# Token chunks of up to 512 columns, no widened copy of the pooled attention, and another split of the weights' rounding

## The chip, the cores and the metric

The kernel runs on one core of a Trainium2 chip. The metric is the device time of one execution in microseconds; of several runs the median counts.

## What is computed

Attention over 8 batches, 8 heads, 576 positions and head dimension 64, and a feed-forward layer on its 4608 tokens. The attention is the sum of two parts: one on `q`, `k`, `v` averaged over groups of four positions, its result repeated four times, and one in which each position sees its neighbours at a distance under 4.

```python
q_d = q.reshape(B, H, Sd, factor, D).mean(axis=3)   # k_d, v_d alike
out_d = sm_attn(q_d, k_d, v_d)
out_up = np.repeat(out_d, factor, axis=2)
mask = np.abs(pos[:, None] - pos[None, :]) < factor
scores = np.where(mask, scale * np.matmul(q, k.transpose(0, 1, 3, 2)), -1e9)
out_local = np.matmul(softmax(scores), v)
x = (out_up + out_local).transpose(0, 2, 1, 3).reshape(B * S, H * D)   # 4608 x 512
h = x @ w_in                      # 512 x 2048
g = np.maximum(0.01 * h, h)
return g @ w_out                  # 2048 x 512
```

## The kernel before

**Number format.** To keep float32 accuracy, each operand of the feed-forward layer is split into a high part (rounded to the format `F32R`) and a low part (what is left), and each product is three matmuls: high by high, low by high, high by low. In the code a trailing `h` or `l` names the part: `gh`, `gl`, `woh`, `wol`; `wi` holds both parts of `w_in`.

**Chunks.** The tokens are columns of all feed-forward matmuls. `plan()` cuts them into `CHUNKS`. Chunk 0 has 512 columns, all of batch 0, whose local attention is made as banded matmuls on TensorE (lines 756 to 831). The other batches are laid out as 9 columns of 64 tokens each (in a batch, "column" j holds the positions that are j modulo 9). `SIZES` gives the number of such columns in each chunk: `(3,) + (6,) * 10`, so chunk 1 has the last 64 tokens of batch 0 and 3 × 64 = 192 more, 256 together, and ten chunks have 384. The last two are made by Strassen's scheme with seven products in place of eight (`finale()`, line 1343).

**Steps.** `STEPS` is the list of feed-forward steps (chunk, first column, last column, f), where f is one of 16 slices of 128 of the 2048 hidden units. A step is twelve up matmuls into a tile `hp` (`up_proj`, line 1060: four slices of x by three products), the leaky ReLU (`leaky`: ScalarE writes `gh` at line 1071 and the exact value at 1072, VectorE the difference `gl` at 1074), and twelve down matmuls into four accumulators of PSUM (`down_proj`, line 1098). Chunk 0 is cut into two halves of 256 columns (`TOP`): the first half runs ahead through f 0 to 7, then the halves alternate, so that the first half is at f + 8 when the second is at f. That spreads over time the moment at which each slice of the weights is first wanted.

**Weights.** `convert(f, k)` makes the parts of slice f of `w_in` (k = 0) or `w_out` (k = 1) from a loaded tile: ScalarE moves the first half word (line 335), VectorE merges it (337), the high part is rounded by ScalarE (348, `w_in`) or by VectorE (345, `w_out`), and the low part is VectorE's subtraction (350). This takes place in the first 120 us, while chunk 0's steps run.

**Local attention of the batches from 1 on.** For each three columns and each half of the heads: GpSimd multiplies q by seven shifted k (line 896), VectorE sums over d (902), some small softmax work follows, GpSimd multiplies by v (969) and VectorE sums (975) into a tile `xloc`. `widen()` lets ScalarE copy the pooled attention's result `outd`, repeated four times, into a tile `up` (line 994, two copies for one part). `landing()` transposes `xloc` on TensorE into a PSUM tile `pt` (1007), adds `up` to it on VectorE (1013), writes the high part of x on ScalarE (1028) and the low part on VectorE (1030):

```python
t = yield from op("DVE", 270 * n, t, tu)
nc.vector.tensor_tensor(out=xv, in0=xv, in1=upv, op=ALU.add)
```

**What sets the order.** All parts are Python generators that run under a planner, the class `Order`. A generator asks for a buffer (`slot`), waits for a named event, and asks for an engine with an estimated duration (`op`); of the generators that are ready, the one with the lowest rank gets the engine next. So the order of every engine's instructions is fixed when the program is built, from estimated costs (`COST`) and ranks; on the chip each engine runs its list in order and waits for semaphores. The x chunks lie in two buffers by parity (`x0`, `x1`), `hp` and `pt` have two each, `gh` and `gl` three each, `xloc` and `prod` two each.

## Time and profile before

| what | value |
|---|---|
| three runs | 911.55, 911.89, 912.01 us |
| their median | 911.89 us |
| profiled execution, span | 910.3 us |
| instructions in the span | 16167 |
| matmuls of 256 columns in up_proj and down_proj | 1152 |
| matmuls of 384 columns in up_proj and down_proj | 3264 |

The profiled execution has no time of its own beside its span; the median of the runs is 1.6 us above that span. PE is TensorE, PEld its weight loads, DVE VectorE, ACT ScalarE, POOL GpSimd, SP SyncE. A row of grouped instructions gives the line, the engine, the operation, the output and input with their shapes, the count, then the busy time in us and the mean ns of one, then the idle time of the engine before them and what ended it. TensorE's rows overlap, since matmuls are pipelined: what one costs is seen from start to start.

### The profile page before, as it was taken

How to read it: one execution, taken by the hardware profiler on the slowest of the kernel's cores; microseconds unless marked ns; L12 is line 12 of the kernel's file. 1: busy time of each engine (PE TensorE's matmuls, PEld its weight loads, DVE VectorE, ACT ScalarE, POOL GpSimd, SP SyncE). 2: the span in 40 equal slices, each digit the busy share in tenths (PEclk: the TensorE clock that was granted, in tenths of full speed). 3: DMA queues.
4: the chain of work that ended last, by engine and by line, in shares of the span. 5: the costliest groups of instructions: out<-in, count | busy, mean ns of one | idle time of the engine just before them, and what ended most of it. 6: DMA issues, size and time to landing. Idle time of an engine off the chain costs nothing. (4 is left out here: it accounts for less than half of the span.)

```text
span 910.3 us, 16167 instructions
## 1 busy us (share of the span) xinstructions
PE 897.6 (99%) x6129; PEld 870.5 (96%) x6129; DVE 610.1 (67%) x887; ACT 460.9 (51%) x1277; POOL 625.9 (69%) x308
## 2 busy tenths in 40 slices
PE   8999999999999999999999999999999999999998
PEld 4789999999999999999999999999999999999998
DVE  6899889888878977875746863762863755533322
ACT  5788567666455634554324553533413425455332
POOL 4221299989989999967974964982993986787100
PEclk9999999999999999999999999999999999999999
DMA  9786566657646644652522751630431410100001
GB/s 294 257 297 240 174 205 207 199 161 216 199 124 200 210 117 121 207 176 64 153 86 76 213 161 27 176 106 27 122 113 45 122 53 1 36 1 1 1 35 36
DMA packets 61774, 119.68 MB, mean 131 GB/s; under 512 B 7248, under 2 KB 24016, under 8 KB 61696
## 3 DMA queue, kind: packets, MB, share of 16 engines
q1 hardware_dynamic: 61696, 118.65, 42.0%
q8 instruction: 48, 0.79, 0.3%
q14 instruction: 30, 0.25, 0.1%
HBM read 109.18 MB, written 9.44 MB: 130 GB/s over the span
## 5 line engine op out<-in xcount | busy, mean ns | idle before, releaser
L1060 PE MATMUL hp<-x,wi 128*128 128x384 f32 (+1 forms) x2112 | 367.4, 323 | 4.5 <-DVE gl L1074 3.6
L1060 PEld LDWEIGHTS hp<-x,wi 128*128 128x128 f32 x2112 | 338.3, 189 | 8.8 <-DVE gl L1074 4.8
L969 POOL TENSOR_TENSOR prod<-v,s 128x1344 f32<-128x1344 f32 x84 | 261.8, 3124 | 62.2 <-DVE xloc L975 57.6
L896 POOL TENSOR_TENSOR prod<-q,k 128x1344 f32<-128x1344 f32 x84 | 265.9, 3171 | 52.7 <-DVE s L902 27.0
L1098 PE MATMUL acc<-gh,woh 128*128 128x384 f32 (+1 forms) x768 | 252.3, 329 | 0.0
L1098 PE MATMUL acc<-gh,wol 128*128 128x384 f32 (+1 forms) x768 | 247.1, 322 | 0.1
L1098 PE MATMUL acc<-gl,woh 128*128 128x384 f32 (+1 forms) x768 | 246.8, 321 | 0.0
L1071 ACT ACTIVATE gh<-hp 128x384 fp32r<-128x384 f32 (+1 forms) x184 | 85.3, 464 | 223.0 <-PE acc L1098 216.8
L1074 DVE TENSOR_TENSOR gl<-hp,gh 128x384 fp32r<-128x384 f32 (+1 forms) x184 | 95.2, 518 | 133.6 <-ACT hp L1072 130.0
L1098 PEld LDWEIGHTS acc<-gh,woh 128*128 128x128 f32 x768 | 144.8, 189 | 2.5 <-issue 2.0
L1098 PEld LDWEIGHTS acc<-gh,wol 128*128 128x128 f32 x768 | 144.8, 188 | 0.5 <-DVE wol L350 0.5
L1098 PEld LDWEIGHTS acc<-gl,woh 128*128 128x128 f32 x768 | 145.0, 189 | 0.0
L902 DVE TENSOR_REDUCE s<-prod 128x21 f32<-128x1344 f32 x84 | 129.3, 1541 | 13.9 <-POOL prod L896 13.9
L975 DVE TENSOR_REDUCE xloc<-prod 128x192 f32<-128x1344 f32 x80 | 123.4, 1543 | 5.1 <-POOL prod L969 5.1
L1072 ACT ACTIVATE hp<-hp 128x384 f32<-128x384 f32 (+1 forms) x184 | 84.4, 459 | 0.0
L1013 DVE TENSOR_TENSOR pt<-pt,up 128x384 f32<-128x384 f32 x42 | 37.6, 895 | 24.6 <-PE pt L1007 22.4
L994 ACT COPY up<-outd 128x576 f32<-128x576 f32 x84 | 52.1, 672 | 0.0
L425 DVE TENSOR_REDUCE v_d<-vs 128x128 f32<-128x512 f32 (+1 forms) x56 | 37.6, 671 | 5.9 <-DMA vs<-in_vrb_dram 5.0
L1028 ACT CAST x<-pt 128x384 fp32r<-128x384 f32 x38 | 18.4, 484 | 35.7 <-DVE pt L1013 35.7
L783 POOL TENSOR_TENSOR xloc<-xloc,lst 128x280 f32<-128x280 f32 (+1 forms) x8 | 7.3, 919 | 27.0 <-ACT pd L512 12.2
L1170 POOL TENSOR_TENSOR sr<-sr 128x256 f32<-128x256 f32 x32 | 23.8, 758 | 0.9
L1170 POOL TENSOR_TENSOR sr<-wi 128x512 f32<-128x512 f32 x16 | 20.6, 1291 | 3.9 <-DVE pt L1013 3.8
(231 smaller groups left out, 1028.4 us busy)
## 6 DMA issues: line engine op xcount, KB each, us to landing
k<-in_kb_dram SPq DMA_DIRECT2D x84, 288.0 KB, 3.3
v<-in_vb_dram SPq DMA_DIRECT2D x84, 288.0 KB, 2.9
qk<-in_qkt_dram SPq DMA_DIRECT2D x32, 576.0 KB, 4.9
q<-in_qb_dram SPq DMA_DIRECT2D x84, 96.0 KB, 2.0
vs<-in_vmb_dram SPq DMA_DIRECT2D x28, 256.0 KB, 2.8
out_dram<-olot SPq DMA_DIRECT2D x36, 192.0 KB, 2.0
...
```

What stands on the lines that cost most here:

```text
L425: nc.vector.tensor_reduce(out=v_d[:rows, k], in_=vs, axis=AX.X, op=ALU.add)
L896: nc.gpsimd.tensor_tensor(out=prv, in0=q[:, a - j0:z - j0].unsqueeze(2).to_broadcast([128, n, W, D]), in1=view(k, (a - j0) * D, [[D, n], [ ...
L902: nc.vector.tensor_reduce(out=s[:, u, p, a - j0:z - j0], in_=prv, axis=AX.X, op=ALU.add)
L969: nc.gpsimd.tensor_tensor(out=prv, in0=view(v, 0, [[1, nj], [nv, D], [1, W]]), in1=s[:, p, :nj].unsqueeze(2).to_broadcast([128, nj, D, W]) ...
L975: nc.vector.tensor_reduce(out=xl_t[:, :nj, p], in_=prv, axis=AX.X, op=ALU.add)
L994: nc.scalar.copy(out=up[:, pp], in_=outd[b][:, 2 * u + pp].unsqueeze(2).to_broadcast([128, SD, FAC]))
L1060: nc.tensor.matmul(hp[:, :n], w[h][:, ws], x[:, c], start=c + j == 0, stop=c == NC - 1 and j == 2)
L1071: nc.scalar.activation(out=gh[:, :n], in_=hp[:, :n], func=AF.Prelu, alpha=0.01)
L1072: nc.scalar.activation(out=hp[:, :n], in_=hp[:, :n], func=AF.Prelu, alpha=0.01)
L1074: nc.vector.tensor_tensor(out=gl[:, :n], in0=hp[:, :n], in1=gh[:, :n].bitcast(F32), op=ALU.subtract)
L1098: nc.tensor.matmul(acc[:, a:z], w[h][:, es], g[:, :n], start=(a, f, j) == (0, 0, 0), stop=f == NF - 1 and j == 2, skip_group_check=ch == 0)
L1170: (nc.vector if eng == "DVE" else nc.gpsimd).tensor_tensor(out=out, in0=in0, in1=in1, op=alu)
```

## The change

1. `SIZES` becomes `(3, 6, 6, 6, 6, 8, 8, 8, 6, 6)`: chunk 1 stays at 256 columns, then come four chunks of 384, three of 512 and the last two of 384. There are 11 chunks in place of 12. Parts of three columns stay, and one may now land in two chunks, so `plan()` keeps for each part the list of its landings. Both x buffers are 512 columns wide; `x1`, which first serves as three staging tiles for the weights, has room for a fourth, and that takes the weights' head tiles.
2. Chunk 0: the first half of the columns runs f 0 to 7 as before. After that, behind each step of the second half for f comes one step of all 512 columns for f + 8. Two half steps share one pair of `gh`, `gl` tiles (`HALF`, `pairs`).
3. `widen()` and its tile `up` are gone. `landing()` adds `outd` to the PSUM tile directly. Since the repeat by four can't be written as one view across a column's tokens, a column takes one or two adds (`RUNS`: 15 for nine columns, 5 for three).
4. `w_out`'s high part is always rounded on ScalarE, and the low parts of the first ten slices (`SHARED`) are subtracted on GpSimd.
5. For Strassen's T4 the buffers are other ones: its two parts lie in what chunk tiles leave free, so that a matmul reads it as three pieces of 128 columns (`Cut`).

```diff
-SIZES = (3,) + (6,) * 10
+SIZES = (3, 6, 6, 6, 6, 8, 8, 8, 6, 6)
...
+SHARED = 10
...
-    parts = {b: [] for b in range(BANDED, B)}
+    parts = {b: [(j, j + MAXSEG, []) for j in range(0, BLK, MAXSEG)] for b in range(BANDED, B)}
     g = 0
     for i, n in enumerate(SIZES):
         mine, z, c0 = [], g + n, 0 if i else S - 512
         while g < z:
             b, j = divmod(g, BLK)
-            room = min(BLK - j, z - g)
-            m = -(-room // -(-room // MAXSEG))
+            _, j1, lands = parts[b + BANDED][j // MAXSEG]
+            m = min(j1 - j, z - g)
             mine.append((b + BANDED, j, j + m, c0))
-            parts[b + BANDED].append((i + 1, j, j + m, c0))
+            lands.append((i + 1, j, j + m, c0))
...
-for f in range(NF):
-    STEPS += [(0, *TOP[1], f)] + [(0, *TOP[0], f + LEAD)] * (f + LEAD < NF)
+for f in range(LEAD):
+    STEPS += [(0, *TOP[1], f), (0, 0, TOP[1][1], f + LEAD)]
...
+HALF = [i for i, (_, a, z, _) in enumerate(STEPS) if z - a == 256]
+HALF = {i: divmod(n, 2) for n, i in enumerate(HALF)}
...
+def runs(j):
+    at = [(BLK * r + j) // FAC for r in range(FAC)]
+    cuts = [0] + [r for r in range(1, FAC) if at[r] != at[r - 1] + 2] + [FAC]
+    return [(r0, r1, at[r0]) for r0, r1 in zip(cuts, cuts[1:])]
+
+
+RUNS = [runs(j) for j in range(BLK)]
...
-    edge_sb = const.tile([128, BLK, W], F32, name="edge_sb")
+    edge_sb = axp.tile([128, BLK, W], F32, name="edge_sb")
...
-    heads = [axp.tile([128, DM], I32, name=f"head{i}") for i in range(bufs["head"])]
+    stage = [wk.tile([128, bufs["stage"] + 1, HALFS * DM], U16, name="x1", tag="x1", bufs=bufs["x1"])]
+    heads = [stage[0][:, bufs["stage"], i * 2 * DM:(i + 1) * 2 * DM].bitcast(I32) for i in range(bufs["head"])]
...
-        s = yield from slot(*(("prod", "up") if f < FREE else ("stage2",) if FSPLIT < f < LSPLIT else ()), "stage")
+        s = yield from slot(*(("prod",) if f < FREE else ("stage2",) if FSPLIT < f < LSPLIT else ()), "stage")
...
-        if k:
-            t = yield from op("DVE", 330, t, lock=True)
-            nc.vector.tensor_copy(out=hi, in_=tf)
+        t = yield from op("ACT", 512, t)
+        nc.scalar.copy(out=hi, in_=tf)
+        if k and f < SHARED:
+            t = yield from op("POOL", 512, t)
+            nc.gpsimd.tensor_tensor(out=lo, in0=tf, in1=hi.bitcast(F32), op=ALU.subtract)
         else:
-            t = yield from op("ACT", 512, t)
-            nc.scalar.copy(out=hi, in_=tf)
-        t = yield from op("DVE", 512, t, lock=True)
-        nc.vector.tensor_tensor(out=lo, in0=tf, in1=hi.bitcast(F32), op=ALU.subtract)
+            t = yield from op("DVE", 512, t, lock=True)
+            nc.vector.tensor_tensor(out=lo, in0=tf, in1=hi.bitcast(F32), op=ALU.subtract)
...
-        both = sb(s_x, [128, 2, NC, XMAX[i % 2]], F32R)[:, :, :, :CHUNKS[i][1]]
+        whole = sb(s_x, [128, 2, NC, 512], F32R)
+        both = whole[:, :, :, :CHUNKS[i][1]]
+        if i == LAST - 1:
+            fin["spare"] = whole[:, :, :, EN:].rearrange("p h c n -> p (h c) n")
...
-        od.spawn(90 + 10 * b + j0 + 0.5 * u, landing(i, b, j0, u, a, z, c0, s_x, xl_t, t))
-
-    ups = {}
-
-    def widen(i, b, j0, j1, u):
-        to = yield from wait(("pooled", b, 2 * u))
-        to = max(to, (yield from wait(("pooled", b, 2 * u + 1))))
-        tx = yield from wait(("xbuf", i))
-        yield from wait(("upturn", ORD[b, j0, u]))
-        s_u = yield from slot("up")
-        od.signal(("upturn", ORD[b, j0, u] + 1))
-        up = sb(s_u, [128, 2, SD, FAC], F32)
-        t = yield from op("ACT", 2 * S, s_u.t, to, times=2)
-        for pp in range(2):
-            nc.scalar.copy(out=up[:, pp], in_=outd[b][:, 2 * u + pp].unsqueeze(2).to_broadcast([128, SD, FAC]))
-        od.signal(("read", b), t)
-        ups[b, j0, u] = up
-        od.signal(("up", b, j0, u), max(t, tx))
-        s_u.free((yield from wait(("upread", b, j0, u), len(pieces(j0, j1)))))
-
-    def landing(i, b, j0, u, a, z, col, s_x, xl_t, t):
+        for k, (i, a, z, col) in enumerate(lands):
+            od.spawn(90 + 10 * b + a + 0.5 * u, landing(i, b, j0, u, a, z, col, s_x, xl_t, t, k == len(lands) - 1))
+
+    def landing(i, b, j0, u, a, z, col, s_x, xl_t, t, last):
         n = z - a
-        tu = yield from wait(("up", b, j0, u))
+        to = max((yield from wait(("pooled", b, 2 * u))), (yield from wait(("pooled", b, 2 * u + 1))))
+        to = max(to, (yield from wait(("xbuf", i))))
         s_b = yield from slot("pt")
         xps = bank(s_b)
         t = yield from pe(0.11 * n, t, s_b.t)
         for m in range(n):
-            nc.tensor.transpose(xps[:, m * 128:(m + 1) * 128], xl_t[:, m].rearrange("p a d -> p (a d)"), id_sb)
-        s_x.free(t)
-        up = ups[b, j0, u]
+            nc.tensor.transpose(xps[:, m * 128:(m + 1) * 128], xl_t[:, a - j0 + m].rearrange("p a d -> p (a d)"), id_sb)
+        if last:
+            s_x.free(t)
         xv = xps[:, :n * 128].rearrange("p (j c t) -> p c j t", j=n, c=2)
-        upv = view(up, a, [[S, 2], [1, n], [BLK, NBLK]])
-        t = yield from op("DVE", 270 * n, t, tu)
-        nc.vector.tensor_tensor(out=xv, in0=xv, in1=upv, op=ALU.add)
-        od.signal(("upread", b, j0, u), t)
+        adds = [(m, *run) for m in range(n) for run in RUNS[a + m]]
+        t = yield from op("DVE", 128 * n, t, to, times=len(adds))
+        for m, r0, r1, o in adds:
+            part = view(xps, m * 128 + r0, [[NBLK, 2], [FAC, NBLK // FAC], [1, r1 - r0]])
+            nc.vector.tensor_tensor(out=part, in0=part, in1=view(outd[b], 2 * u * SD + o, [[SD, 2], [BLK, NBLK // FAC], [2, r1 - r0]]), op=ALU.add)
+        od.signal(("read", b), t)
...
+    pairs = {}
+
     def leaky(i, n, s_h, hp, t):
-        s_g, s_l = (yield from slot("gh")), (yield from slot("gl"))
-        gh, gl = sb(s_g, [128, OMAX], F32R), sb(s_l, [128, OMAX], F32R)
+        pair, second = HALF.get(i, (None, 0))
+        if second:
+            yield from wait(("pair", pair))
+            s_g, s_l, gh, gl = pairs.pop(pair)
+        else:
+            s_g, s_l = (yield from slot("gh")), (yield from slot("gl"))
+            gh, gl = sb(s_g, [128, OMAX], F32R), sb(s_l, [128, OMAX], F32R)
+            if i in HALF:
+                pairs[pair] = s_g, s_l, gh[:, n:], gl[:, n:]
+                od.signal(("pair", pair))
...
-            s_g.free(t)
-            s_l.free(t)
+            if HALF.get(i, (0, 1))[1]:
+                s_g.free(t)
+                s_l.free(t)
...
+        hi, lo, src = fin["t4"], fin["spare"][:, :6], raw[0, 1].rearrange("p c (k n) -> p (c k) n", n=512 - EN)
+        t = yield from halve(hi, lo, src, 2 * EN, "DVE", t, tx)
+        T["T4"] = [Cut(x, EN // (512 - EN)) for x in (lo, hi)]
...
+                        acc = held[b][1][:, :EN]
+                        if x == "T4":
+                            acc = acc.rearrange("p (k n) -> p k n", n=512 - EN)
+                        nc.tensor.matmul(acc, w[h][:, c * 128:(c + 1) * 128], T[x][m][:, c],
```

In the numbered lines of the changed kernel, the lines that are named above move as follows: up matmul 1060 to 1057, down matmul 1098 to 1105, `gl` 1074 to 1081, score product 896 to 907, score sum 902 to 913, merge 337 to 347, low part 350 to 360 (on GpSimd 357).

TensorE in the middle of chunk 0. `wi_77`, `woh_83` and `wol_82` belong to a slice f of the first nine, the tiles with numbers over 1000 to slices from 9 on. Before:

```order
L1098 MATMUL acc_599<-gh,woh_1046 128x256
L1098 MATMUL acc_599<-gl,woh_1046 128x256
L1098 MATMUL acc_599<-gh,wol_1045 128x256
L1060 MATMUL hp<-x_103,wi_77 128x256 x12
L1060 MATMUL hp<-x_103,wi_1043 128x256 x12
L1098 MATMUL acc_630<-gh,woh_1046 128x256
L1098 MATMUL acc_630<-gl,woh_1046 128x256
L1098 MATMUL acc_630<-gh,wol_1045 128x256
```

and now:

```order
L1057 MATMUL hp<-x_101,wi_1051 128x512 x12
L1057 MATMUL hp<-x_101,wi_76 128x256 x6
L503 MATMUL pt<-qblk_87 96x144 x3
L1057 MATMUL hp<-x_101,wi_76 128x256 x6
L1105 MATMUL acc_593<-gh,woh_1056 128x512
L1105 MATMUL acc_593<-gl,woh_1056 128x512
L1105 MATMUL acc_593<-gh,wol_1055 128x512
L1105 MATMUL acc_620<-gh,woh_1056 128x512
```

The steps for f from 8 on now have 512 columns, and their down matmuls follow each other where the two halves took turns.

GpSimd where the batches' scores begin (`xloc` and `lst` belong to batch 0's banded part, `edge_sb` masks the ends). Before:

```order
L783 TENSOR_TENSOR xloc<-xloc,lst 128x350 x4
L896 TENSOR_TENSOR prod<-q,k 128x1344 x5
L915 TENSOR_TENSOR s<-s,edge_sb 128x84
L896 TENSOR_TENSOR prod<-q,k 128x1344
L922 TENSOR_TENSOR s<-s,st_l 128x84
L896 TENSOR_TENSOR prod<-q,k 128x1344
L932 TENSOR_TENSOR s<-s,st_l 128x84
L969 TENSOR_TENSOR prod<-v,s 128x1344
```

and now:

```order
L796 TENSOR_TENSOR xloc<-xloc,lst 128x350 x2
L357 TENSOR_TENSOR wol_82<-prod,woh_83 128x512
L357 TENSOR_TENSOR wol_82<-x_84,woh_83 128x512
L907 TENSOR_TENSOR prod<-q,k 128x1344
L357 TENSOR_TENSOR wol_82<-x_84,woh_83 128x512
L357 TENSOR_TENSOR wol_82<-prod,woh_83 128x512
L907 TENSOR_TENSOR prod<-q,k 128x1344
L357 TENSOR_TENSOR wol_1055<-x_84,woh_1056 128x512
L907 TENSOR_TENSOR prod<-q,k 128x1344 x3
L926 TENSOR_TENSOR s<-s,edge_sb 128x84
```

Low parts of `w_out` stand between the last additions of batch 0 and among the first products.

VectorE at the first score sum of batch 1. Before:

```order
L337 SCALAR_TENSOR_TENSOR x_102<-x_102,head_85 128x512
L1074 TENSOR_TENSOR gl<-hp,gh 128x256
L345 CAST woh_1436<-x_102 128x512
L350 TENSOR_TENSOR wol_1435<-x_102,woh_1436 128x512
L457 TENSOR_REDUCE qk<-qk 128x144
L850 TENSOR_TENSOR x_1547<-olot,x_1547 128x4x64
L425 TENSOR_REDUCE v_d<-vs 128x128
L902 TENSOR_REDUCE s<-prod 128x21
```

and now:

```order
L913 TENSOR_REDUCE s<-prod 128x21
L347 SCALAR_TENSOR_TENSOR x_84<-x_84 128x512
L347 SCALAR_TENSOR_TENSOR prod<-prod,x_84 128x512
L522 TENSOR_REDUCE st_d<-pt 96x3
L1081 TENSOR_TENSOR gl<-hp,gh 128x512
L534 RECIPROCAL st_d<-st_d 96x3
L1081 TENSOR_TENSOR gl<-hp,gh 128x256
L360 TENSOR_TENSOR wi_1050<-x_84,wi_1050 128x512
L347 SCALAR_TENSOR_TENSOR stage_1060<-stage_1060,x_84 128x512
L347 SCALAR_TENSOR_TENSOR x_84<-x_84 128x512
L913 TENSOR_REDUCE s<-prod 128x21
L360 TENSOR_TENSOR wi_1051<-stage_1060,wi_1051 128x512
```

Before, the first score sum stood behind all merges and low parts of the weights. Now the first two stand among them, over 60 places further ahead.

## Rows read from the trace of the kernel before

**Rows 1.** The page's top: span and busy time of each engine.
```profile
span 910.3 us, 16167 instructions
...
PE 897.6 (99%) x6129; PEld 870.5 (96%) x6129; DVE 610.1 (67%) x887; ACT 460.9 (51%) x1277; POOL 625.9 (69%) x308
```
**Rows 2.** The page's slices: granted TensorE clock, tenths of full speed.
```profile
PEclk9999999999999999999999999999999999999999
```
**Rows 3.** Whom PE waited for: us in total, times, longest us.
```profile
PE hp L1060 <- DVE gl L1074: 3.6, 4, 1.4
...
PE hp L1060 <- DVE wi L350: 0.8, 2, 0.5
```
**Rows 4.** The chain that ended last, in time order: start us, us, work.
```profile
772.50 8.32 PE acc L1098 x48
```
**Rows 5.** PE timeline, 38.8 to 40.3 us: start us, us, instruction.
```profile
38.86 0.28 PE L1098 MATMUL acc<-gh,woh 128*128 128x256 f32 x1
...
40.18 0.28 PE L1098 MATMUL acc<-gh,wol 128*128 128x256 f32 x1
```
**Rows 6.** PE timeline, 9 to 13 us, the warm-up matmuls.
```profile
9.07 0.60 PE L313 MATMUL acc<-band_sb,idb_sb 128*128 128x512 bf16 x2
...
12.53 0.38 PE L313 MATMUL acc<-band_sb,idb_sb 128*128 128x512 bf16 x1
```
**Rows 7.** Groups by shape: busy us, mean ns of one, idle before.
```profile
L994 ACT COPY up<-outd 128x576 f32<-128x576 f32 x84 | 52.1, 672 | 0.0
L1013 DVE TENSOR_TENSOR pt<-pt,up 128x384 f32<-128x384 f32 x42 | 37.6, 895 | 24.6 <-PE pt L1007 22.4 <-ACT olot L1140 1.1 <-ACT up L994 0.6
...
L1261 DVE TENSOR_TENSOR hp<-hp,sp 128x384 f32<-128x384 f32 x12 | 6.7, 566 | 13.1 <-ACT sp L1255 13.0
...
L690 DVE RECIPROCAL st_d<-st_d 112x3 f32<-112x3 f32 x16 | 2.7, 166 | 0.2 <-ACT st_d L688 0.2
...
L345 DVE CAST woh<-x 128x512 fp32r<-128x512 f32 x7 | 3.0, 423 | 0.0
...
L350 DVE TENSOR_TENSOR wol<-x,woh 128x512 fp32r<-128x512 f32 x7 | 4.8, 686 | 0.0
...
L348 ACT CAST wi<-x 128x512 fp32r<-128x512 f32 x9 | 5.9, 660 | 0.6 <-DVE x L337 0.4
...
L1170 POOL TENSOR_TENSOR sr<-wi 128x512 f32<-128x512 f32 x16 | 20.6, 1291 | 3.9 <-DVE pt L1013 3.8
```
**Rows 8.** Stretches: busy us (x) of PE, PEld, DVE, ACT, POOL; clock, DMA, GB/s.
```profile
60.00:80.00 20.00, 19.85 (x178) 19.37 (x177) 18.89 (x35) 17.45 (x49) 7.15 (x2) 1.00 0.88 321
80.00:100.00 20.00, 20.00 (x168) 19.98 (x167) 18.47 (x35) 14.10 (x29) 0.00 (x0) 1.00 0.40 133
```
**Rows 9.** DVE timeline, 67 to 80 us.
```profile
67.99 1.18 DVE L350 TENSOR_TENSOR wi<-x,wi 128x512 fp32r<-128x512 f32 x1
...
78.61 1.36 DVE L337 SCALAR_TENSOR_TENSOR x<-x,head 128x512 int32<-128x512 int32 x1 [0.28 <-ACT head L335]
79.89 0.68 DVE L337 SCALAR_TENSOR_TENSOR stage<-stage,head 128x512 int32<-128x512 int32 x1
```
**Rows 10.** POOL timeline, 60 to 110 us; in brackets the idle time before.
```profile
65.07 3.55 POOL L896 TENSOR_TENSOR prod<-q,k 128x1344 f32<-128x1344 f32 x1 [6.46 <-DVE wi L350]
75.82 3.59 POOL L896 TENSOR_TENSOR prod<-q,k 128x1344 f32<-128x1344 f32 x1 [7.20 <-DVE wol L350]
105.67 3.14 POOL L896 TENSOR_TENSOR prod<-q,k 128x1344 f32<-128x1344 f32 x1 [26.25 <-DVE s L902]
```
**Rows 11.** DVE timeline: the last low parts of x for chunks 1 and 2.
```profile
148.35 0.55 DVE L1030 TENSOR_TENSOR x<-pt,x 128x384 fp32r<-128x384 f32 x1
...
202.94 0.55 DVE L1030 TENSOR_TENSOR x<-pt,x 128x384 fp32r<-128x384 f32 x1
```
**Rows 12.** PE timeline: the first up matmuls of chunks 1 and 2.
```profile
148.78 1.48 PE L1060 MATMUL hp<-x,wi 128*128 128x256 f32 x11
...
204.02 1.21 PE L1060 MATMUL hp<-x,wi 128*128 128x384 f32 x6
```
**Rows 13.** Who waited for whom, all engines.
```profile
POOL prod L969 <- DVE xloc L975: 57.6, 8, 13.3
```

More of the change, by code (lines that the diff above doesn't have):

```diff
@@ L362, in outd_tile @@
         od.signal(("outd", b), s.t)
-        t = yield from wait(("read", b), 8 if b < BANDED else 2 * len(PARTS[b]))
+        t = yield from wait(("read", b), 8 if b < BANDED else 2 * sum(len(p[2]) for p in PARTS[b]))
         s.free(t)
@@ L858, in attn_moe @@
     state = {}
[L859 to L860 removed]
+    ORD = {(b, a, u): 2 * k + u for k, (b, a) in enumerate((b, p[0]) for b in PARTS for p in PARTS[b]) for u in range(2)}
+    for name in ("turn", "ask", "vask"):
         od.signal((name, 0))
@@ L1163, in make_room @@
         od.signal(("xbuf", LAST), t)
-        t = yield from wait("landed", len(ORD))
+        t = yield from wait("landed", sum(LANDED[i, 0] for i in range(1, LAST + 1)) - 1)
         at.__exit__(None, None, None)
@@ L1218, in split_x31 @@
         yield from wait(("over", LAST - 2))
-        s_x = yield from slot("x1")
-        pair = sb(s_x, [128, 2, 2, 2, EN], F32R)
+        s_x = yield from slot(f"x{LAST % 2}")
+        whole = sb(s_x, [128, 10, EN], F32R)
+        pair = whole[:, :8].rearrange("p (k m c) n -> p k m c n", k=2, m=2)
+        fin["t4"] = whole[:, 8:].rearrange("p c (k n) -> p (c k) n", n=512 - EN)
+        od.signal("x1free", s_x.t)
         for k, (j, h) in enumerate((("T3", 0), ("T1", 1))):
```

87 lines of the change are left out of this document (40 added, 47 removed).

## The prediction

> **What bounds the kernel now.** I read the page's top first. TensorE is busy 897.6 of 910.3 us [rows 1]; VectorE, ScalarE and GpSimd are at 51 to 69%. The granted clock is full in all forty slices [rows 2], so TensorE ran at the higher of its two levels, 2.4 GHz, throughout, and no gain or loss is to be looked for there. Next, who TensorE waited for [rows 3]: VectorE's low half of g (`gl`) for 3.6 us and the low part of a `w_in` tile for 0.8 us, both in the steps of chunk 0, and hardly anything after. The chain that ended last is therefore almost all matmuls; one link of it is 48 down-projections of 384 columns back to back in 8.32 us [rows 4]. So the time is the sum of TensorE's matmuls, and the question is what one costs as a function of its columns.
>
> That is read from starts, because durations of pipelined matmuls overlap. Twelve 256-column matmuls start at 38.86 ... 40.18 us, eleven steps in 1.32 us: **120 ns** from start to start [rows 5]. The 48 of 384 columns take 8.32/48 = **173.3 ns** each [rows 4]. The difference, 53.3 ns for 128 columns, is 2.4 columns per ns. What is left at either size, 120 − 106.7 and 173.3 − 160, is **13.3 ns** that a matmul costs however wide it is.
>
> **The change, part by part.**
>
> *Wider chunks and a chunk fewer.* In the two programs I counted the up and down matmuls. Before: 1152 of 256 columns and 3264 of 384. After: 768 of 256, 1728 of 384 and 1344 of 512. The columns are the same (1,548,288), the matmuls are 576 fewer, and nothing else on TensorE changes in number. The price of 512 columns isn't shown for float32 rows. Below: a warm-up pair of bfloat16 lasts 0.60 us and a single one 0.38 [rows 6], so the second adds 0.22 us; above: two of 256, 240 ns, which would be no gain. The straight line through 256 and 384 gives 213.3 + 13.3 = 226.7 ns, near the warm-up pair, and I take it.
> Before 1152 × 120 + 3264 × 173.3 = 704.0 us; after 768 × 120 + 1728 × 173.3 + 1344 × 226.7 = 696.3. **−7.7 us**, which is 576 × 13.3. With 220 ns the gain would be 16.7 us, with 240 the kernel would lose 10.2; but nothing in the rows speaks for a bend of the line right behind two points that both leave 13.3 ns, so of these ends I keep ±2 us in the main case and the rest as rival 4.
> One page of the Trainium skill speaks against this: "TensorE: Matmul & The Clock Gate", section "Wait — 56ns, not 53.3ns?", puts the start-to-start time of warm matmuls at columns/2.4 GHz plus about 2.5 ns. By that rule 576 matmuls fewer would give 1.4 us. The trace doesn't agree: 13.3 ns are left at both sizes [rows 4, 5].
>
> *Chunk 0's halves.* Of these 7.7 us, 192 of the 512-column matmuls lie in chunk 0: eight up and eight down steps now run once over all columns (384 × 120 + 192 × 226.7 = 89.6 in place of 768 × 120 = 92.2 us). So chunk 0 is 2.6 us shorter, and everything that it needs and that comes behind it is wanted earlier by up to that.
>
> *No widened copy.* ScalarE loses 84 copies, 52.1 us (the first row of [rows 7]). In their place VectorE's 42 adds of 0.895 us (its second row) become five small adds for three columns. The row does not show their price. An add of 384 columns with one operand in PSUM takes 566 ns (its third row), one tiny instruction 166 ns (its fourth). Below: 5 × 166 ns + 384 × 1.05 ns = 1.23 us, where 1.05 ns is (566 − 166)/384, rounded up; above, with the old add's (895 − 166)/384 = 1.90 ns, 5 × 166 + 730 = 1.56 us. That is +14 to +28 us on VectorE in all, spread from the first landing to the last on an engine that is 67% busy [rows 1], and on no chain that TensorE waits for, so **0** as long as x stays ahead (rival 2).
>
> *w_out's rounding and low parts.* In the setup's 60 us, VectorE loses sixteen roundings of 423 ns and ten subtractions of 686 ns [rows 7]: 16 × 0.42 + 10 × 0.69 = 13.7 us. ScalarE gains 16 × 0.66 = 10.6 us; GpSimd gains ten subtractions of a 128×512 tile, 1.29 us each by a row of its own (the last of [rows 7]) = 12.9 us. VectorE is the engine that is full here: 18.89 of 20 us and 18.47 of 20 in the two stretches of 60 to 100 us, with ScalarE at 17.45 and 14.10 and GpSimd at 7.15 and 0.00 [rows 8]. GpSimd waited 6.46, 7.20 and 26.25 us between its first products [rows 10], the last for score reductions that stood behind VectorE's conversions. So the relief is on the right engine. At most it ends the 4.4 us of [rows 3]. But chunk 0 asks for the weights of f 8 to 15 by full rows now, and the planner fills VectorE's room with score reductions that used to come after the last conversion. I take **0** for it, and leave −4.4 as an end.
>
> *The Strassen end.* T4 moves into spare columns of the x tiles and is read as three pieces of 128 columns within one matmul; the matmuls keep their number and width. Its additions are the same instructions. 0.
>
> The sum: −7.7. The profiled span is 910.3 us, 1.6 below the runs' median of 911.9, which I take as what lies around the span. 911.9 − 7.7 = **904.2 us**.
>
> **The rivals.**
>
> 1. *The start's waits go as well.* VectorE's 13.7 us of relief ends the waits of [rows 3]: −7.7 − 4.4, **899.8 us**. For it: `gl` is late in just the stretch where VectorE is full. Against it: the freed time is planned full again.
>
> 2. *x comes just in time.* Chunk 1's last low part starts at 148.35 and takes 0.55, while chunk 1's first matmul starts at 148.78; for chunk 2 it is 202.94 + 0.55 against 204.02 [rows 11, 12]. Neither has slack to give. If the local attention comes no sooner, the 2.6 us of chunk 0 turn into a wait ahead of chunk 1 or 2: 904.2 + 2.6 = **906.8 us**. Against it: GpSimd and VectorE lose the conversions' queue, and further on GpSimd waits 57.6 us for buffers [rows 13], so from chunk 3 on the supply is far ahead.
>
> 3. *The other side: VectorE and GpSimd in each other's way.* While GpSimd's product of 65.07 + 3.55 ran, VectorE's subtraction at 67.99 took 1.18 us instead of 0.69 and ended 0.55 us behind it; at 78.61 a merge of halves took 1.36 instead of the next one's 0.68 and ended 0.56 us behind the product of 75.82 + 3.59 [rows 7, 9, 10]. Both products ran 0.4 us over the 3.14 of the third. The change puts ten subtractions and about eight products on GpSimd among VectorE's conversions: 12.9 + 8 × 3.14 = 38.0 us in which VectorE could stand still, against 13.7 us of relief. Half of that, 19.0, costs 19.0 − 13.7 = 5.3 us: 904.2 + 5.3 = 909.5; three quarters, 28.5, costs 14.8: **919.0 us**. It decides, and the kernel is slower, if VectorE loses more than 13.7 + 7.7 = 21.4 of the 38.0 us and TensorE's waits from 60 to 125 us grow by as much. For it: VectorE, at 18.9 of 20 us [rows 8], has no room. Against: of TensorE's waits only 0.8 us were for a weight [rows 3], so most weights come before they are wanted, and the first part of a delay is hidden.
> The Trainium skill says so in "SBUF — State Buffer", section "Who interferes with whom": a VectorE instruction with two SBUF operands and a GpSimd instruction that reads SBUF take one pair of ports, whoever begins first holds it for the whole instruction, and the other waits. The two rows at 67.99 and 78.61 agree with it.
>
> 4. *The width takes the saving back.* The 13.3 ns are saved only if a 512-column matmul has no fixed part larger than the narrower ones. At 226.7 + 7.7 us/1344 = 232.4 ns, halfway between the line and two of 256, nothing is left: **911.9 us**, the same as before. For it: no float32 row of 512 columns is there to exclude it. Against it: two sizes agree to 0.1 ns, and the bfloat16 pair's 0.22 us is under the line. By the rule of the Trainium skill that is named above, too, there would be no change that can be measured, 911.9 − 1.4 = 910.5 us.
>
> **How the numbers follow.** A difference of 0.2%, 1.8 us, is about the least that a measurement of this kernel can tell from none. The main case (902.5 to 906.5) gets 0.50: TensorE is at 99%, and the gain is arithmetic on its own rows. Rival 1 gets 0.14, rival 2 0.22, rival 3 0.10 (0.07 of it slower, 0.02 within the bound, 0.01 faster) and rival 4 0.04. Faster 0.50 + 0.14 + 0.22 + 0.01 = 0.87, same 0.06, slower 0.07. The range takes in the main case and rival 2 with half of rival 1 and the mild end of rival 3: 900.5 to 909.0; it leaves out the rest of rivals 1 and 3, and rival 4, some 0.18 in all.
>
> **What would show it.** Right: 512-column matmuls start 227 ns apart, TensorE's busy time is near 890 us, its waits stay near 10 us, no copy to `up` on ScalarE, and the five adds together take 1.2 to 1.6 us. Rival 1: no wait of TensorE for `gl` or `wi` before 150 us. Rival 2: a TensorE wait for a low part of x of 2 to 3 us ahead of chunk 1 or 2. Rival 3: VectorE instructions of twice their usual length that end just behind a GpSimd instruction, and TensorE waits for `wi`, `wol` or `gl` of over 7 us between 60 and 125 us. Wrong altogether: a pitch at 512 columns of 235 ns or more, or TensorE waits of over 15 us at any place.

## The result: slower by 1.2%

The changed kernel takes 922.79 us (median of four runs, 920.65 to 924.83); the kernel before 911.72 beside it. The ratio is 1.0123, with an interval of 1.011 to 1.0136. The forecast was 904.2 us, with 909.0 as its upper end.

The page's top after the change, against [rows 1]:

```profile
span 920.8 us, 15049 instructions
...
PE 899.6 (98%) x5553; PEld 811.9 (88%) x5553; DVE 630.8 (69%) x1009; ACT 416.6 (45%) x1161; POOL 641.1 (70%) x318
```

There are 576 fewer matmuls, as counted, yet TensorE is busy 2.0 us longer than before in place of some 7.7 shorter, and the span is 10.5 us longer. First the price of a matmul of 512 columns, from TensorE's timeline between 603 and 606 us:

```profile
603.28 0.39 PE L1105 MATMUL acc<-gh,wol 128*128 128x512 f32 x1
...
606.00 0.39 PE L1105 MATMUL acc<-gh,wol 128*128 128x512 f32 x1
```

Twelve steps in 2.72 us are 226.7 ns, the value taken from the straight line. So the gain is there, and something else takes more. Whom TensorE waited for, in us, times and longest, against [rows 3]:

```profile
PE hp L1057 <- DVE gl L1081: 10.2, 9, 2.9
...
PE acc L1105 <- ACT olot L1148: 1.1, 1, 1.1
```

VectorE's `gl` was waited for 10.2 us in place of 3.6, and 5.1 us of that lie between 60 and 150 us:

```profile
PE hp L1057 <- DVE gl L1081: 5.1, 3, 2.3
PE hp L1057 <- DVE wi L360: 0.4, 1, 0.4
```

How it is spread, the stretches show (busy us of PE, PEld, DVE, ACT, POOL; granted clock; DMA). First before, then after:

```profile
60.00:150.00 90.00, 88.73 (x764) 87.37 (x763) 80.72 (x136) 64.28 (x192) 47.52 (x20) 1.00 0.62 204
150.00:250.00 100.00, 99.30 (x768) 97.02 (x767) 88.88 (x123) 61.15 (x199) 93.35 (x39) 1.00 0.65 202
250.00:760.00 510.00, 509.56 (x3182) 500.28 (x3182) 337.50 (x426) 225.86 (x630) 403.15 (x170) 1.00 0.40 121
```

```profile
60.00:150.00 90.00, 84.38 (x540) 73.60 (x538) 80.99 (x107) 63.28 (x178) 48.00 (x21) 0.96 0.60 198
150.00:250.00 100.00, 97.00 (x738) 93.35 (x735) 88.78 (x149) 53.76 (x186) 89.88 (x38) 0.98 0.62 193
250.00:760.00 510.00, 507.40 (x2836) 453.07 (x2836) 363.72 (x568) 192.94 (x549) 419.58 (x181) 1.00 0.41 123
```

TensorE's idle time in the three is 1.3, 0.7 and 0.4 us before, and 5.6, 3.0 and 2.6 after: 8.8 us more. VectorE's busy time behind 250 us is 26 us longer. And the clock is no longer full. Around TensorE's wait of 1.8 us that ends at 87.81:

```profile
86.00:88.00 2.00, 0.19 (x1) 0.19 (x2) 2.00 (x3) 1.20 (x4) 2.00 (x2) 1.00 0.56 226
88.00:90.00 2.00, 2.00 (x7) 1.57 (x7) 2.00 (x3) 1.09 (x3) 2.00 (x1) 0.69 0.00 0
90.00:92.00 2.00, 2.00 (x6) 1.51 (x6) 1.91 (x3) 0.00 (x0) 0.16 (x1) 0.50 0.84 270
92.00:94.00 2.00, 2.00 (x17) 1.96 (x16) 0.11 (x1) 1.52 (x3) 0.00 (x0) 0.96 0.89 216
```

The share 0.50 is the lower level, 1.2 GHz, while TensorE is busy all the time. The loss is 2 × (0.31 + 0.50 + 0.04) = 1.7 us, nearly the wait over again. The same follows the waits of 2.3 us that ends at 136.84 and of 2.9 us that ends at 217.61, so the three falls cost some 5.1 us. Matmuls −7.7, idle time +8.8, clock +5.1 make +6.2 of the 10.5 us. The other 4.3 us don't lie in waits elsewhere: outside the three stretches TensorE is idle for 10.3 us before (12.7 in all) and 10.0 after (21.2 in all). They are inside its busy time. I take them for many small delays that the modelled ends of the matmuls cover, and don't divide them.

VectorE's conversions of the weights, in its timeline, against [rows 9]:

```profile
75.65 2.67 DVE L360 TENSOR_TENSOR wi<-x,wi 128x512 fp32r<-128x512 f32 x1
...
82.92 4.24 DVE L347 SCALAR_TENSOR_TENSOR stage<-stage,x 128x512 int32<-128x512 int32 x2
87.08 0.68 DVE L1081 TENSOR_TENSOR gl<-hp,gh 128x512 fp32r<-128x512 f32 x1
...
106.85 3.31 DVE L347 SCALAR_TENSOR_TENSOR x<-x 128x512 int32<-128x512 int32 x1 [0.25 <-ACT x L345]
...
127.52 3.52 DVE L347 SCALAR_TENSOR_TENSOR x<-x 128x512 int32<-128x512 int32 x1
...
133.68 2.51 DVE L360 TENSOR_TENSOR wol<-x,woh 128x512 fp32r<-128x512 f32 x1
```

and GpSimd's, against [rows 10]:

```profile
74.60 3.17 POOL L907 TENSOR_TENSOR prod<-q,k 128x1344 f32<-128x1344 f32 x1
...
82.92 7.24 POOL L907 TENSOR_TENSOR prod<-q,k 128x1344 f32<-128x1344 f32 x2
...
106.17 3.44 POOL L907 TENSOR_TENSOR prod<-q,k 128x1344 f32<-128x1344 f32 x1 [16.01 <-DMA k<-in_kb_dram]
...
127.34 3.14 POOL L907 TENSOR_TENSOR prod<-q,k 128x1344 f32<-128x1344 f32 x1
132.58 3.06 POOL L980 TENSOR_TENSOR prod<-v,s 128x1344 f32<-128x1344 f32 x1 [2.09 <-DVE xloc L986]
```

Each of these long conversions begins while a product runs and ends 0.55 to 0.56 us behind it (75.65 + 2.67 = 78.32 against 74.60 + 3.17 = 77.77; of the two products from 82.92 on, the first ends at 86.61, the second merge at 87.16). Over all conversions longer than 0.8 us, the time above the usual 0.69 is 14.6 us for ten of them; before it was 1.2 us for two. Six stand under products and have 13.5 of the 14.6 us; the other four, of 0.82 to 1.09 us between 40 and 59 us, end as far behind shorter additions and subtractions of GpSimd. That is the picture of rival 3, though its second sign is not met: TensorE's waits for `gl` and `wi` between 60 and 125 us are 3.2 us, not over 7. The `gl` of 87.08 stands behind the 4.24 us, and TensorE's wait up to 87.81 behind that `gl`.

### The profile page after: what moved, and what is told of

It is laid out like the page before. It is cut to its first block, busy times and chain, and to the rows that moved or that the text cites. A ratio compares the mean times of both kernels' runs of the same rounds, so it can differ in the third digit from the quotient of the medians.

```text
span 920.8 us, 15049 instructions
## 1 busy us (share of the span) xinstructions
PE 899.6 (98%) x5553; PEld 811.9 (88%) x5553; DVE 630.8 (69%) x1009; ACT 416.6 (45%) x1161; POOL 641.1 (70%) x318
## 4 chain that ended last, share of the span: by engine, by line
PE 84%; DVE 8%; ACT 3%; DMA 3%; issue 2%; SPq 0%; ACTq 0%; DVEq 0%
PE acc L1105 34%; PE hp L1057 33%; PE pt L1362 5%; PE hp L1362 2%; PE hp L1105 2%; PE pt L1105 2%; PE pt L1002 1%; DVE gl L1081 1%; DVE pt L1010 1%; DVE xloc L986 1%; DMA prod<-in_w_in_dram 1%; PE pt L503 1%; DVE x L347 1%; PE pt L652 1%; DMA qk<-in_qkt_dram 1%
## 5 line engine op out<-in xcount | busy, mean ns | idle before, releaser
L1057 PE MATMUL hp<-x,wi 128*128 128x384 f32 (+2 forms) x1824 | 367.5, 351 | 11.1 <-DVE gl L1081 10.2
L1057 PEld LDWEIGHTS hp<-x,wi 128*128 128x128 f32 x1824 | 308.7, 190 | 47.0 <-DVE gl L1081 17.3
L1105 PE MATMUL acc<-gh,woh 128*128 128x384 f32 (+2 forms) x672 | 235.4, 350 | 1.1 <-ACT olot L1148 1.1
L1105 PE MATMUL acc<-gh,wol 128*128 128x384 f32 (+2 forms) x672 | 230.8, 343 | 0.0
L1105 PE MATMUL acc<-gl,woh 128*128 128x384 f32 (+2 forms) x672 | 230.6, 343 | 0.0
L1078 ACT ACTIVATE gh<-hp 128x384 fp32r<-128x384 f32 (+2 forms) x160 | 81.3, 508 | 192.4 <-PE acc L1105 182.2
L1081 DVE TENSOR_TENSOR gl<-hp,gh 128x384 fp32r<-128x384 f32 (+2 forms) x160 | 91.0, 571 | 101.8 <-ACT hp L1079 99.6
L1010 DVE TENSOR_TENSOR pt<-pt,outd 128x64 f32<-128x64 f32 (+3 forms) x210 | 53.9, 259 | 40.2 <-PE pt L1002 33.7
L1079 ACT ACTIVATE hp<-hp 128x384 f32<-128x384 f32 (+2 forms) x160 | 80.6, 504 | 0.0
L1027 DVE TENSOR_TENSOR x<-pt,x 128x384 fp32r<-128x384 f32 (+2 forms) x42 | 21.4, 513 | 2.4 <-ACT x L1025 1.4
L1148 ACT COPY olot<-acc 128x384 f32<-128x384 f32 (+2 forms) x34 | 16.7, 503 | 13.9 <-PE acc L1105 7.2
```

What stands on the lines that cost most here:

```text
L1010: nc.vector.tensor_tensor(out=part, in0=part, in1=view(outd[b], 2 * u * SD + o, [[SD, 2], [BLK, NBLK // FAC], [2, r1 - r0]]), op=ALU.add)
L1057: nc.tensor.matmul(hp[:, :n], w[h][:, ws], x[:, c], start=c + j == 0, stop=c == NC - 1 and j == 2)
L1078: nc.scalar.activation(out=gh[:, :n], in_=hp[:, :n], func=AF.Prelu, alpha=0.01)
L1079: nc.scalar.activation(out=hp[:, :n], in_=hp[:, :n], func=AF.Prelu, alpha=0.01)
L1081: nc.vector.tensor_tensor(out=gl[:, :n], in0=hp[:, :n], in1=gh[:, :n].bitcast(F32), op=ALU.subtract)
L1105: nc.tensor.matmul(acc[:, a:z], w[h][:, es], g[:, :n], start=(a, f, j) == (0, 0, 0), stop=f == NF - 1 and j == 2, skip_group_check=ch == 0)
```

## The experiments

All times are medians; the kernel before gave 910.9 to 911.1 in these runs and 911.72 beside the changed kernel, so that a difference to the changed kernel can be up to 0.8 us too large.

### The price of 512 columns

`sizes384` cuts the chunks behind chunk 1 as before.

```diff
-SIZES = (3, 6, 6, 6, 6, 8, 8, 8, 6, 6)
+SIZES = (3,) + (6,) * 10
...
-OMAX = max(c[1] for c in CHUNKS[1:])
+OMAX = max(c[1] for c in CHUNKS)
```

> The changed kernel with ten chunks of 384 columns behind chunk 1, as before; chunk 0 keeps its 512-column steps. Up to the end of chunk 5 the work is the same. If the 13.3 ns per matmul are real at 512 columns, the 384 matmuls more cost 5.1 us, and the time is 926 to 930 us. If the wider chunks gain nothing (their waits or the halves of a landing take it back), it is within 2 us of 922.8, or faster.

929.8 us (925.8 to 931.1), 7.0 more than the changed kernel and in the range that the 13.3 ns gave. The wider chunks do gain; that all of the 7.0 us are matmuls is not shown, since the landings change too (384 × 13.3 ns are 5.1 us). With the 226.7 ns from start to start, rival 4 is out.

### GpSimd's products among the conversions

`memset` leaves the order as it is and the first eight products of batch 1 out: GpSimd writes a constant in their place and reads nothing.

```diff
+            if b == BANDED and j0 < 6:
+                nc.gpsimd.memset(pr[:, :nj * W * D], 0)
+            else:
                 nc.gpsimd.tensor_tensor(
                     out=prv,
...
```

> The changed kernel with the same order of instructions on every engine, but the eight score products of batch 1's first six columns are left out: GpSimd writes a constant into the product tile in their place, which reads nothing. Theory A (a GpSimd product that reads SBUF holds VectorE's two-operand instructions until its end): the conversions of 2.0 to 3.6 us at 75.65, 83.52, 88.67, 106.85 and 127.52 us fall to about 0.7, only the one at 133.68 (under a value product) stays; TensorE's waits from 60 to 150 us fall from 5.6 to under 3 us and the time from 922.8 to 914 to 918 us. Rival: the order alone makes the waits (score sums ahead of gl on VectorE); then the conversions get short, but the waits stay above 4.5 us and the time above 919.5.

914.84 us (1.0024 to 1.0052 of before): 8.0 us less. VectorE's pair of conversions and its `gl`, and GpSimd's pair above it, now read:

```profile
83.44 1.28 DVE L347 SCALAR_TENSOR_TENSOR stage<-stage,x 128x512 int32<-128x512 int32 x2
85.18 0.69 DVE L1084 TENSOR_TENSOR gl<-hp,gh 128x512 fp32r<-128x512 f32 x1 [0.45 <-ACT hp L1082]
```

```profile
83.44 2.38 POOL L908 MEMSET prod<- 128x1344 f32 x2
```

The pair takes 1.28 us in place of 4.24, though GpSimd is busy above it. TensorE's waits between 60 and 150 us fall from 5.7 to 1.8 us, none of them for `gl`, at the full clock; the time above 0.69 falls from 14.6 to 2.9 us.

```profile
PE pt L1005 <- DVE st_l L934: 1.4, 1, 1.4
PE hp L1060 <- DVE wi L360: 0.4, 1, 0.4
```

With the order the same, the order alone is not the cause. The memset is also shorter than a product (1.2 us for about 3.2), so a part of the 8.0 us may come from that; but the conversions are released even while it runs.

`scores_late` (n = 26) and `late20` (n = 20) hold the products back and leave nothing out.

```diff
         yield from wait(("ask", ORD[b, j0, u]))
+        yield from wait("converted", n)
```

> The changed kernel, but no score product of the batches from 1 on is issued before 26 of the 32 weight conversions are done. Theory A (GpSimd's score products lock VectorE's conversions, which end up to 3 us late, and so does gl): VectorE's conversions over 0.8 us lose at least 10 of their 14.6 us above the usual 0.69, TensorE's waits between 60 and 150 us fall from 5.6 us to under 2.5 with the full clock there, and the time falls from 922.8 to 914 to 918 us. Theory B (the late join of chunk 0's halves itself leaves too little room for gl, products or not): the waits stay above 4 us and the time within 2 us of 922.8. A miss of another kind: batch 1's x comes later and TensorE waits for it at the start of chunk 1.

> The changed kernel with no score product before 20 of the 32 conversions are done (26 gave 916.6 us, with 4.5 us of waits for x near 151 us). Theory A: a hold that is shorter leaves x in time and still keeps most products apart from the conversions: TensorE's waits near 151 us under 2 us, long conversions under 6 us, 912 to 916 us. Rival: with the products back among the conversions the waits before 150 us come back, 917 to 921 us.

`scores_late`: 916.57 us. TensorE's waits from 60 to 150 us fall to 0.8, and the time above 0.69 from 14.6 to 5.2 us, 9.4 less and so just short of the 10 that was asked. The miss that was named came too, TensorE waiting near 151 us for chunk 1's x (first line) and near 153 for the pooled attention (second):

```profile
PE pt L1003 <- DVE xloc L987: 3.2, 1, 3.2
...
PE pt L503 <- ACT qblk L474: 1.3, 1, 1.3
```

`late20`: 920.36 us, the rival's range: 9.2 us above 0.69 are left, TensorE waits 4.7 us from 60 to 150 us (3.2 of them for the pooled attention's `qblk`, 1.1 for `gl`), and 2.7 us for x behind that. A hold trades one wait for the other.

`before_early` does the opposite to the kernel before.

```diff
-                    od.spawn(89 + r, scores(b, j0, j1, u))
+                    od.spawn(89 + r - (90 if b == BANDED and j0 == 0 else 0), scores(b, j0, j1, u))
```

> The kernel before with one number changed: batch 1's first score products get a rank ahead of the weights' conversions, so that they and their sums stand among the conversions (the first three sums some 60 places further ahead on VectorE). Nothing of the change is in it. Theory A (products among conversions lock VectorE, whatever else is changed): VectorE's conversions over 0.8 us rise from 1.2 to over 6 us above the usual 0.69, and the time from 911 to 915 to 921 us. Rival (the late join or the lost staging tiles are needed for the loss): within 2 us of 911.

935.97 us, far above the expected range. The time above 0.69 of the merges and low parts is 7.8 us, as expected, but the waits are mainly others:

```profile
PE hp L1060 <- DVE wi L350: 6.4, 6, 2.2
PE pt L490 <- ACT qblk L461: 4.1, 2, 3.1
PE hp L1060 <- DVE gl L1074: 3.4, 3, 1.6
PE acc L1098 <- DVE woh L345: 2.5, 1, 2.5
```

Products and sums ahead of the conversions make the weights late in themselves. So it shows how little room there is, not what the lock costs.

### The split of w_out

Four ways: `lows_dve` sets `SHARED = 0` (only the rounding stays moved), `lows_pool` takes the rounding back (only the low parts stay moved), `round_dve` does both.

```diff
-SHARED = 10
+SHARED = 0
...
-        t = yield from op("ACT", 512, t)
-        nc.scalar.copy(out=hi, in_=tf)
+        if k:
+            t = yield from op("DVE", 330, t, lock=True)
+            nc.vector.tensor_copy(out=hi, in_=tf)
+        else:
+            t = yield from op("ACT", 512, t)
+            nc.scalar.copy(out=hi, in_=tf)
```

> The changed kernel with the ten low parts of w_out subtracted on VectorE again (ScalarE still rounds). Theory A, in which the score products and not these ten short instructions do the locking: VectorE has 6.9 us more to do before 120 us, the long conversions stay, 921 to 927 us. Rival: the low parts on GpSimd were what held VectorE; then the long conversions go and the time falls by 4 us or more.

> The changed kernel with w_out's rounding back on VectorE but the ten low parts left on GpSimd: the fourth of the four ways to split this work (both moved 922.8, only the rounding moved 918.2, none moved 912.7 us). Theory A: VectorE is full enough to keep most score sums back, but three stand among the conversions now and GpSimd's low parts lie there too; long conversions 4 to 10 us, 914 to 920 us. Rival: if the low parts on GpSimd were harmless relief, 909 to 912.5.

> The changed kernel with the split of w_out as before: rounding and low parts on VectorE. Chunk 0 keeps its late join. If part 4 of the change is what spoils chunk 0 (it frees VectorE for score sums, and so GpSimd for products that lock it), the score sums go back behind the conversions, TensorE's waits and lowered clock from 60 to 150 us cost under 5 us in place of 11.4, and the time is 912 to 917 us. If the late join is what needs the weights too early, VectorE is now later still and the time is 920 to 928.

| rounding | low parts | time | conversions, time above 0.69 |
|---|---|---|---|
| ScalarE | GpSimd (the change) | 922.8 | 14.6 |
| ScalarE | VectorE (`lows_dve`) | 918.2 (913.9 to 919.7) | 9.4 |
| VectorE | GpSimd (`lows_pool`) | 919.5 | 5.4 |
| VectorE | VectorE (`round_dve`) | 912.7 | 3.2 |

To undo the relief of VectorE makes the kernel 10.1 us faster. In `round_dve` the first score sum stands again behind all conversions. `lows_dve` went the rival's way by its time, but its long conversions stay, 9.4 us of them under products; for the low parts alone it settles nothing. `lows_pool` loses its time mainly at chunk 1, where x comes 3.1 us late: from 60 to 150 us TensorE waits for only 0.6 us.

### The late join of chunk 0's halves

`halves` runs chunk 0 in halves to the end; `halves_lows` also has `SHARED = 0`; `halves_round` also the rounding on VectorE.

```diff
-for f in range(LEAD):
-    STEPS += [(0, *TOP[1], f), (0, 0, TOP[1][1], f + LEAD)]
+for f in range(NF):
+    STEPS += [(0, *TOP[1], f)] + [(0, *TOP[0], f + LEAD)] * (f + LEAD < NF)
...
-        s_x.free((yield from wait(("done", i))))
+        s_x.free((yield from wait(("done", i), 2 if i == 0 else 1)))
```

> The changed kernel with chunk 0 in alternating halves of 256 columns to the end, as before. TensorE's matmuls cost 2.6 us more (192 more of them at 13.3 ns). Theory A: conversions and products still stand among each other, TensorE's waits between 60 and 150 us stay above 3.5 us; 922 to 927 us. Theory B: the waits at 87.8, 114.7 and 136.8 us (5.1 us together) and the lowered clock behind them go; 914 to 919 us.

> The changed kernel with chunk 0 in halves to the end and the ten low parts of w_out on VectorE; ScalarE still rounds w_out. Against the halves alone (918.2 us) the first score sum stands 38 places further back on VectorE. Theory A: long conversions under 4 us in all, 60 to 150 us cost under 5 us above the matmuls' price, time 910 to 916 us. Rival: no better than the halves alone, 917 to 920.

> The changed kernel with two parts undone: chunk 0 in halves to the end, and w_out's rounding and low parts on VectorE. What is left of the change is three chunks of 512, no widened copy, the landing in small adds. The matmuls gain 384 x 13.3 ns = 5.1 us on the kernel before. If the loss sits in chunk 0 alone, the time is 905 to 909 us, faster than both kernels. If the small adds and the landings over two chunks also delay gl later on, 910 to 915.

918.2, 922.2 and 918.6 us. By its time and by the waits that went (those for `gl` between 60 and 150 us fall from 5.1 to 0.7 us), `halves` came out as theory B had it. But its order is another one, too: the second score sum stands behind most of the conversions, and the time above 0.69 falls to 5.6 us, so this run doesn't tell the theories apart. `halves_lows` lies above both ranges that were named for it, with runs from 919.7 to 927.7.

With w_out's split moved, the halves are 4.6 us faster than the late join; with the split on VectorE, 5.9 us slower, of which 2.6 are the matmuls and the rest is not explained. So the late join alone is not the cause: `round_dve` has it too, and waits for no `gl` from 60 to 150 us. `halves_round` was to be faster than both kernels if the loss sat in chunk 0, and is not: TensorE waits 5.1 us for `gl` in eleven places, all over the kernel, which pointed away from chunk 0.

### The five small adds

`one_add` (on `round_dve`) and `after_one_add` (on the changed kernel) keep the order and land with a single add; `both_out` is `memset` and `after_one_add` together.

```diff
-        for m, r0, r1, o in adds:
-            part = view(xps, m * 128 + r0, [[NBLK, 2], [FAC, NBLK // FAC], [1, r1 - r0]])
-            nc.vector.tensor_tensor(out=part, in0=part, in1=view(outd[b], 2 * u * SD + o, [[SD, 2], [BLK, NBLK // FAC], [2, r1 - r0]]), op=ALU.add)
+        nc.vector.tensor_tensor(out=xv, in0=xv, in1=view(outd[b], 2 * u * SD, [[SD, 2], [BLK, n], [1, NBLK]]), op=ALU.add)
```

> The changed kernel with w_out's rounding and low parts on VectorE (912.7 us), the same order, but a landing adds the pooled part in one instruction of 384 columns from a stretch of outd that isn't repeated by four (the repetition is left out). Theory C: the five small adds keep gl waiting behind 250 us, where this kernel spends 4 us more above the matmuls' price than the kernel before; then that falls by 2 us or more and the time to 909 to 911 us. Rival: the adds are hidden, as the prediction had it: 911.5 to 913.5 us.

> The changed kernel, same order, with one add of 384 columns in a landing in place of five small ones (the repetition by four is left out). If the adds cost here what they cost on the kernel with w_out's split undone (6.3 us), 915.5 to 918 us. If the locked conversions hide them, above 920.

> The changed kernel, same order, with batch 1's first eight score products left out (a constant is written) and one add in a landing (the repetition by four is left out). If the two causes add up, 914.8 - 6.3 = 908.5 us, between 907 and 910; with the waits that the kernel before has too, that would be the forecast of 904.2 up to some 4 us. If they overlap, 911 to 914.

`one_add` 906.37 us (0.994 to 0.997 of before): 6.3 less than `round_dve`. `after_one_add` 912.77: 10.0 less than the changed kernel, more than was expected; its ten runs go from 911.5 to 916.4, and by the ratios to the kernel before it is 8.7 less. `both_out` 908.89: 13.9 less. The two causes, 8.0 and 10.0, overlap by 4.1 us; together they are three quarters of the miss of 18.6.

Most of the overlap has a place. In the profiled executions both `memset` and `after_one_add` lack the two falls of the clock before 150 us, 3.4 us. In `after_one_add` TensorE's idle time there stays nearly as it was, 5.4 us against 5.6:

```profile
60.00:150.00 90.00, 84.56 (x563) 74.19 (x562) 81.43 (x110) 65.47 (x182) 52.58 (x23) 1.00 0.63 205
```

A wait of 1.8 us that ends at 87.64 is still among it, and this time the clock stayed full. That this is due to the adds is not shown, so up to 3.4 of the 10.0 us are not theirs for certain; `one_add` against `round_dve`, with the full clock there in both profiled executions, gives 6.3. The adds in the changed kernel, grouped by shape (busy us, mean ns):

```profile
L1010 DVE TENSOR_TENSOR pt<-pt,outd 128x96 f32<-128x96 f32 x56 | 15.7, 280 | 1.9
L1010 DVE TENSOR_TENSOR pt<-pt,outd 128x64 f32<-128x64 f32 x56 | 14.0, 250 | 18.4 <-PE pt L1002 16.9
L1010 DVE TENSOR_TENSOR pt<-pt,outd 128x128 f32<-128x128 f32 x42 | 12.5, 299 | 8.1 <-PE pt L1002 6.3 <-ACT st_d L695 0.5 <-issue 0.4
L1010 DVE TENSOR_TENSOR pt<-pt,outd 128x32 f32<-128x32 f32 x56 | 12.0, 218 | 11.9 <-PE pt L1002 10.5
```

54.2 us for 42 parts of three columns are 1.29 us each, within the 1.23 to 1.56 that were worked out, and 16.6 us more than the old adds of [rows 7]. The single add in `one_add` (four more have 256 columns):

```profile
L1012 DVE TENSOR_TENSOR pt<-pt,outd 128x384 f32<-128x384 f32 x38 | 21.1, 564 | 31.9 <-PE pt L1006 30.6 <-ACT hp L1081 0.8 <-ACT st_d L699 0.5
```

How a landing reaches TensorE shows in `round_dve`, VectorE's timeline before a wait of 0.7 us of TensorE at 544.09:

```profile
542.02 1.42 DVE L1014 TENSOR_TENSOR pt<-pt,outd 128x32 f32<-128x32 f32 x5
543.35 0.68 DVE L1085 TENSOR_TENSOR gl<-hp,gh 128x512 fp32r<-128x512 f32 x1
```

The five adds stand just ahead of a `gl` for which TensorE waits, and the planner reckons them at 5 × 0.08 + 384 × 0.00104 = 0.8 us. `true_cost` (on `round_dve`) tells it 1.4; `true_cost_late` also holds the products back with n = 24.

```diff
-        t = yield from op("DVE", 128 * n, t, to, times=len(adds))
+        t = yield from op("DVE", 128 * n, t, to, times=2.5 * len(adds))
```

> The changed kernel with w_out's split on VectorE (912.7 us), where the planner reckons a landing's five adds at 1.4 us, as measured, in place of 0.8. Nothing is left out. If the 6.3 us come from a plan that puts the adds ahead of gl because it takes them for shorter, most of it is won back: 907 to 910 us, faster than the kernel before. If VectorE's time itself is what lacks, 911 to 914 us.

> As true_cost, and no score product is issued before 24 of the 32 conversions are done. The two products that still stand among the conversions go behind them (the long conversion of 3.6 us near 71 us goes, and TensorE's wait of 1.0 us near 76 with it), but x of chunk 1 comes later. Theory A: within 2 us of true_cost, to either side, since what is won near 76 us is lost near 150.

`true_cost` 909.81 us (0.9976 to 0.9996 of before): 2.9 less than `round_dve`, nothing left out. From 250 to 900 us no wait for `gl` over 0.1 us is left, and TensorE's idle time from 250 to 760 us, 2.7 us in `round_dve` (first line), is 0.3 as before the change (second line, `true_cost`):

```profile
250.00:760.00 510.00, 507.30 (x2830) 452.61 (x2829) 361.65 (x562) 195.74 (x559) 419.94 (x185) 1.00 0.40 122
250.00:760.00 510.00, 509.67 (x2856) 457.73 (x2855) 364.03 (x565) 195.20 (x555) 420.86 (x182) 1.00 0.39 122
```

VectorE is busy in it for 364 us, as in the changed kernel and no less than in `round_dve`: the 2.9 us come from the new order, not from shorter adds. The other 3.4 us that `one_add` gains are not won back by this plan, and whether they are the adds' length stays open. `true_cost_late` 915.12: the theory's ±2 us missed, since TensorE waits 5.8 us near 155 us for the pooled attention and chunk 1's x, and the clock of 150 to 250 us falls to 0.95. `true_cost` is the one complete version that beats both kernels, though by 0.1% only, less than the difference that the prediction called measurable.

## Why the prediction was wrong

- **The price of a matmul** was right: 226.7 ns, 576 fewer, at full clock. The 2.5 ns of the Trainium skill ("TensorE: Matmul & The Clock Gate", section "Wait — 56ns, not 53.3ns?") don't hold for these rows; the trace has 13.3 ns at 512 columns too (226.7 − 213.3).
- **"w_out's rounding and low parts: I take 0."** The first step that failed. The relief did what the order of instructions showed, score sums among the conversions, but I priced only the relief, and gave what follows, products of GpSimd beside conversions, 0.10 as rival 3. Its mechanism is shown by `memset`; its price was mis-sized: 8.0 us in place of 0. The Trainium skill says in "SBUF — State Buffer", section "Who interferes with whom", that a VectorE instruction with two SBUF inputs contends with a GpSimd instruction that reads SBUF, not with one that only writes it. The trace agrees on both counts: 4.24 us for two merges under products, 1.28 under memsets. VectorE lost 14.6 of the 38.0 us, below the 21.4 that were to decide, and the kernel was slower all the same. The threshold set lost time of VectorE against relief in one sum, by which 14.6 us would have cost 0.9. But the relief was already spent on score sums, and what counts is when one conversion blocks the `gl` behind it, and the fall of the clock that can follow.
- **"No widened copy: 0."** The second. The length of the adds was right (1.29 us), but "on no chain that TensorE waits for" was judged by VectorE's share of 67%. An engine at 67% still delays `gl` when the plan puts adds that it takes for 0.8 us in front of it. Without them the changed kernel is 10.0 us faster, in part together with the first cause, and `round_dve` 6.3, of which a right estimate alone wins 2.9.
- **"No gain or loss is to be looked for" in the clock.** The third. It held for the kernel before, whose longest wait for `gl` is 1.4 us [rows 3]. Behind three waits of 1.8 to 2.9 us the clock fell to the lower level and cost 1.7 us more each time.
- **"Chunk 0's halves", −2.6 us:** with the split back on VectorE the late join was worth 5.9 us, on the changed kernel −4.6. Its price depends on the rest of the order, and only its 2.6 us of matmuls are explained.
- **Rival 2** (x just in time) came where products were held back or came late: `scores_late`, `late20`, `lows_pool`, `true_cost_late`, and `halves` too. It is the reason why a hold doesn't simply take the first cause away. **Rival 1** is out: no version of the start lost its waits.
- Two sums of the prediction are off in the last digit (16.6 for its 16.7 us at 220 ns, 13.6 for its 13.7 us of relief); neither changes anything.
- What is left of the miss, 908.9 of `both_out` against 904.2, is in good part one place: the wait for `gl` that ends at 217.61 in the changed kernel stays there, 2.6 us at 209.53, with a fall of the clock beside it. In the changed kernel ScalarE stood 2.3 us before a copy of chunk 1's output:

```profile
212.74 0.37 ACT L1148 COPY olot<-acc 128x256 f32<-128x256 f32 x1 [2.32 <-DMA out_dram<-olot]
```

It waited for the store of an earlier piece to free an output tile, and the leaky ReLU stood behind it until 214.61; it was done at 215.47. That is only the first part of TensorE's wait. VectorE's list has another reduction ahead of that `gl`, and it waited for a load:

```profile
216.34 0.75 DVE L467 TENSOR_REDUCE qblk<-qk 128x144 f32<-128x576 f32 x1 [1.42 <-DMA qk<-in_qkt_dram]
217.01 0.55 DVE L1081 TENSOR_TENSOR gl<-hp,gh 128x384 fp32r<-128x384 f32 x1
```

Neither the store nor the load was tried, so this part stays argued.
